# Window attention beside a gated feed-forward: the 8 KB transfer of the negated maxima is issued by GpSimd instead of SyncE

## The chip, the core and the metric

One core of one Trainium2 chip runs the whole program. The metric is the device time of one execution in microseconds; less is better. The time before is 872.02 us, the median of three runs (869.25 to 873.17).

## What is computed

The input x has 2048 tokens of 512 values. It is normed over each token, and two branches read the normed tokens:

```python
def _A_ref(x, wqkv, wo):            # 32 heads of 16, window of 256 tokens
    q, k, v = ...                   # x @ wqkv, split by head
    scores = jnp.einsum("bhqd,bhkd->bhqk", q, k) * (Dh ** -0.5)
    mask = (idx[:, None] - idx[None, :] >= 0) & (idx[:, None] - idx[None, :] < W)
    p = _softmax(jnp.where(mask[None, None], scores, -1e9), axis=-1)
    return (p @ v) @ wo
def _B_ref(x, w_gate, w_up, w_down):
    return (_silu(x @ w_gate) * (x @ w_up)) @ w_down
s = _A_ref(xn, A_wqkv, A_wo)
g = _silu(_B_ref(xn, B_w_gate, B_w_up, B_w_down))
return x + s * g
```

All data is float32.

## The kernel before

The tokens are cut into 4 chunks of 512. For each chunk the dense work on TensorE is: projections of queries and keys (tiles `a`), values (`vp`), gate and up (`g`, `u`), down (`d`) and the output projection (`s`). All of it goes through `next_mm`, and its matmuls stand on line 470. Each product is made of three, since every operand is split into a rounded part and a rest (`xh` and `xl`, `wh` and `wl`, `hh`). The rest of the weights, `wl`, is a GpSimd subtraction on line 434 that follows ScalarE's rounding on line 429. The rest of the hidden values, `hh`, is one on line 628.

Attention is made in 32 units u, 8 groups of 4 heads in each chunk. One unit goes through these steps:

1. `load_qk` brings its queries and keys from DRAM into the tiles `q` and `k` (SyncE's queue, tiles used in rotation by three).
2. `max_pair`: 16 score matmuls `b` (line 970), and for each a masked row maximum on VectorE (line 978) into one column of the tile `m`.
3. `max_turn`: two small transposes `mt` on TensorE (line 1004, first one half of the rows, then the other) turn the columns of maxima into rows.
4. `neg` (line 1019, ScalarE): the maxima, negated, go to the 16 x 128 tile `ms`. `put` then copies `ms` with one 8 KB DMA into row 48 and row 112 of the unit's `q` tile. Row 48 of the `k` tile holds ones, so that a product over 49 rows is score minus maximum.
5. `prob_pair`: matmuls `c` over 49 rows (line 1121), the exponential on ScalarE (`p`, line 1082), and the masks on the tile `p` by GpSimd (lines 1095 and 1099), one instruction for each masked block: 12 a unit in the first chunk, 16 in the others. The last two masks of a unit belong to its last pair of heads.
6. `pv_visit`: all products of `p` and `v` in one go (line 1158), which needs every mask of the unit.
7. The result goes to DRAM (`od`), is divided by the sums (`den`, `rd`) and comes back as the tile that `Wo` reads (`o`, lines 893 and 906).

The order of instructions on each engine is not written by hand. The program holds a planner, which runs while the kernel is built: it keeps a virtual clock, one queue of ready work for each of VectorE, ScalarE, GpSimd and DMA, and a cost for each piece. `do(engine, ready, cost, ...)` puts a piece in a queue and reports its end to a callback. `dma(...)` does the same for the queue of SyncE, with at most 8 transfers under way, a rate by size and 3.5 us (`LAND`) to landing. At each step the planner gives TensorE the dense matmul that is next, or an attention step whose inputs are ready by the virtual clock and whose due time has come. So a cost that is changed at one place changes the order of TensorE, ScalarE, VectorE, GpSimd and SyncE from there on. Each engine then runs its list in order on the chip, and waits on semaphores.

For the step at hand: `after_neg` is called when `neg` is done by the virtual clock. It queues `put`, and `ms_at[u]` is when the planner takes the maxima as landed. `prob_ready` asks for `ms_at[u]`, so it decides when the first `c` of the unit may be placed. The due times of `max_turn` and of the first `prob_pair` of a unit are 0.27 of a unit apart. The second transpose `mt` of unit u+1 (due at u + 1.8) stands close to `pv_visit` of unit u (due at u + 1.89).

Of the kernel before, what the change touches and what calls it, by code (L numbers as in the profile page):

```python
# [55 lines left out]
def tile_window_attention_swiglu_gate(  # L56
# [10 lines left out]
    nc = tc.nc  # L67
# [16 lines left out]
    def sb(name, shape, dtype, kind, n):  # L84
        return pers.tile(shape, dtype, name=name, tag=ring(kind, n), bufs=1)

    def f32(ap):
        return ap.bitcast(F32)

    def move(dst, src, eng=nc.sync):  # L90
        if dst.dtype == F32R:
            dst = f32(dst)
        if src.dtype == F32R:
            src = f32(src)
        eng.dma_start(dst, src)  # L95
# [11 lines left out]
    def do(e, ready, cost, fn, then=None, slack=0.5, can=None, lat=None):  # L107
        seq[0] += 1
        queue[e].append((ready + slack, seq[0], ready, cost, fn, then, can, LAT.get(e, 0.0) if lat is None else lat))
# [5 lines left out]
    def dma(ready, fn, then=None, slack=0.5, kb=256, can=None, e="D"):  # L115
        def begun_at(t):
            stream_at[0] = max(stream_at[0], t) + kb / 230.0
            done = stream_at[0] + LAND
            lanes.append(done)
            lanes.pop(0)  # L120
            if then:
                then(done)

        do(e, ready, 0.5, fn, begun_at, slack, lambda: lanes[0] <= now[0] and (can is None or can()), 0.0)
# [52 lines left out]
    def bank(pool, name):  # L177
        tag = min((v, k) for k, v in pool.items() if v is not None)[1]
        pool[tag] = None
        return ps.tile([P, 512], F32, name=name, tag=tag, bufs=1), tag  # L180
# [5 lines left out]
    qs = [pers.tile([P, 2, TC], F32R, name=f"q{i}") for i in range(3)]  # L186
# [168 lines left out]
    def half(r):  # L355
        return slice(R * r, R * r + R)
# [109 lines left out]
    def handover(pb):  # L466
        nc.vector.tensor_copy(pers.tile([MW, 1], F32, name="ho", tag=ring("ho", 2), bufs=1), pb[:MW, 0:1])
# [457 lines left out]
    ms_at = {}  # L925
# [72 lines left out]
    def max_turn(u, r):  # L998
        if r == 0:
            mtp[u] = [*bank(rb_free, f"mt{u}"), None]  # L1000
        pb, tag, _ = mtp[u]

        def go():
            nc.tensor.matmul(
                pb[:MW, R * r : R * r + R], mts[u % 2][half(r), :], ident[half(r), half(r)],
                is_transpose=True, start=True, stop=True,
            )

        if r == 0:
            def after(t):  # L1010
                mtp[u][2] = t

            extra[0].append((128, go, lambda t: do("V", t, 0.09, lambda: handover(pb), after, -1.0)))
            return
        box = []

        def neg():
            box.append(sb(f"ms{u}", [16, P], F32R, "ms", 2))
            nc.scalar.activation(box[0], pb[:16, :P], AF.Copy, scale=-1.0)

        def after_neg(t):
            rb_free[tag] = t
            dma(t, put, lambda t: ms_at.__setitem__(u, t + 1.0), -3.0, 8)

        def put():
            move(qs[u % 3][48 : 113 : 64], box[0])

        extra[1].append((128, go, lambda t: do("S", t, 0.25, neg, after_neg, -1.0)))

# [372 lines left out]
    while True:  # L1403
# [15 lines left out]
        if not any(extra):  # L1419
            s = work[0] / PACE - LEAD  # L1420
            for st in sorted(streams, key=lambda st: st[-1][0] if st else 1e9):
# [7 lines left out]
                t = need(*a)  # L1429
# [20 lines left out]
        if os.environ.get("VIRT"):  # L1450
            u, i = stream[min(pos[0], len(stream) - 1)]
# [40 lines left out]
```

## Time and profile before

| | us |
|---|---|
| median of three runs | 872.02 |
| the profiled execution, its time | 870.93 |
| its span on the core | 869.2 |
| TensorE matmul busy (PE) | 858.0 |
| GpSimd busy (POOL) | 638.1 |
| ScalarE busy (ACT) | 506.2 |
| VectorE busy (DVE) | 486.0 |

In the rows of the profile PE is TensorE's matmul, PEld its weight load, DVE VectorE, ACT ScalarE, POOL GpSimd, and SPq the queue of SyncE, which issues the DMAs. A row of the timeline has the start, the duration, the engine, the line, the operation, the tiles (out<-in, numbers left out), the shapes and a count; in brackets is the idle time of the engine before it, and what ended that. A row of the waits has the waiting instruction, what ended the wait, the sum in us, how often, and the longest. TensorE's clock was granted in full (0.999).

### The profile page before, as it was taken

What the parts mean: (1) busy time and instruction counts of PE and PEld (TensorE: products, weight loads), DVE (VectorE), ACT (ScalarE), POOL (GpSimd) and SP (SyncE); (2) the same over time, 40 slices, a digit from 0 to 9 for tenths busy, and PEclk for the clock granted to TensorE, in tenths of its full rate; (3) what the DMA queues carried; (4) which work ended last, traced back from release to release, by engine and by line L of the source; (5) the groups of instructions that cost most, each with busy time, mean ns of one, the idle gap of its engine ahead of it and who ended that gap; (6) DMA issues with size and microseconds to landing.
All of it is one profiled execution on the core that took longest, in us unless ns stands there. A gap on an engine that the chain in (4) does not pass through costs nothing.

```text
span 869.2 us, 30153 instructions
## 1 busy us (share of the span) xinstructions
PE 858.0 (99%) x11960; PEld 789.8 (91%) x11960; DVE 486.0 (56%) x1627; ACT 506.2 (58%) x1074; POOL 638.1 (73%) x888
## 2 busy tenths in 40 slices
PE   9999999999999999999999999999999999999997
PEld 8799999898889899989999989898999989999897
DVE  4364466655646655666555765565655566554233
ACT  4355565555665567565576666665656765566532
POOL 6576575668796776767799695676758997769774
PEclk9999999999999999999999999999999999999999
DMA  5785855466877985664767897556657779744342
GB/s 141 192 197 124 222 117 162 116 173 167 198 160 187 253 182 115 141 158 109 202 140 194 219 229 171 124 149 143 174 129 185 154 171 217 167 124 112 108 123 78
DMA packets 69489, 139.63 MB, mean 161 GB/s; under 512 B 14546, under 2 KB 23250, under 8 KB 69348
## 3 DMA queue, kind: packets, MB, share of 16 engines
q1 hardware_dynamic: 69060, 137.18, 63.9%
q8 instruction: 94, 1.54, 0.8%
q10 hardware_dynamic: 288, 0.52, 0.2%
q14 instruction: 47, 0.39, 0.2%
HBM read 107.74 MB, written 29.62 MB: 158 GB/s over the span
## 4 chain that ended last, share of the span: by engine, by line
PE 87%; DMA 8%; POOL 2%; SPq 1%; DVE 1%; issue 1%; ACT 1%; DVEq 0%; ACTq 0%; POOLq 0%
PE d L470 17%; PE u L470 15%; PE g L470 15%; PE a L470 11%; PE pv L1158 8%; PE s L470 5%; PE c L1121 5%; PE vp L470 4%; PE b L970 4%; DMA wr<-wo 2%; DMA k<-qkd 1%; POOL wl L434 1%; DMA den<-od 1%; DMA qkd<-qkl 1%; SPq L95 1%; DMA wr<-wqk 1%
## 5 line engine op out<-in xcount | busy, mean ns | idle before, releaser
L434 POOL TENSOR_TENSOR wl<-wr,wh 128x512 fp32r<-128x512 f32 (+2 forms) x258 | 306.8, 1207 | 101.1 <-ACT wh L429 91.9
L978 DVE CUSTOM_DVE_ANT_0 jk<-b,maskb 128x384 bf16<-128x384 f32 (+2 forms) x512 | 271.8, 531 | 132.5 <-PE b L970 71.5
L1082 ACT ACTIVATE p<-c 128x384 f32<-128x384 f32 (+1 forms) x480 | 208.2, 490 | 105.1 <-PE c L1121 89.0
L470 PE MATMUL d<-wh,hh 64*128 64x256 f32 x1792 | 259.3, 278 | 0.0
L470 PEld LDWEIGHTS d<-wh,hh 64*128 64x128 f32 x1792 | 227.1, 185 | 0.9 <-issue 0.6
L470 PE MATMUL d<-wl,hh 64*128 64x256 f32 x896 | 207.8, 279 | 0.0
L429 ACT ACTIVATE wh<-wr 128x512 fp32r<-128x512 f32 (+2 forms) x258 | 142.0, 594 | 65.5 <-PE d L470 16.0
L470 PE MATMUL u<-xh,wh 64*128 64x512 f32 x448 | 170.0, 396 | 0.0
L470 PE MATMUL g<-xh,wh 64*128 64x512 f32 x448 | 169.7, 395 | 0.0
L470 PE MATMUL u<-xl,wh 64*128 64x512 f32 x448 | 169.6, 396 | 0.0
L470 PE MATMUL g<-xl,wh 64*128 64x512 f32 x448 | 169.1, 395 | 0.0
L470 PE MATMUL u<-xh,wl 64*128 64x512 f32 x448 | 168.9, 395 | 0.0
L470 PE MATMUL g<-xh,wl 64*128 64x512 f32 x448 | 168.9, 395 | 0.0
L470 PEld LDWEIGHTS d<-wl,hh 64*128 64x128 f32 x896 | 154.9, 185 | 0.3
L1095 POOL TENSOR_SCALAR_AFFINE_SELECT p<-p 128x256 f32<-128x256 f32 x256 | 103.4, 408 | 57.1 <-ACT p L1082 54.0
L970 PE MATMUL b<-k,q 48*128 48x384 f32 (+1 forms) x512 | 116.6, 334 | 2.7 <-DMA k<-qkd 1.4
L1121 PE MATMUL c<-q,k 49*128 49x384 f32 (+1 forms) x704 | 111.7, 306 | 2.0 <-ACT p L1082 1.0
L1099 POOL TENSOR_SCALAR_AFFINE_SELECT p<-p 128x256 f32<-128x256 f32 x224 | 91.2, 409 | 11.4 <-ACT p L1082 9.6
L628 POOL TENSOR_TENSOR hh<-h,hh 128x512 fp32r<-128x512 f32 x56 | 72.5, 1295 | 36.4 <-ACT hh L624 30.1
L470 PE MATMUL a<-xh,wl 64*128 64x512 f32 (+1 forms) x264 | 97.0, 385 | 0.0
L470 PE MATMUL a<-xh,wh 64*128 64x512 f32 (+1 forms) x264 | 96.8, 390 | 0.0
L470 PE MATMUL a<-xl,wh 64*128 64x512 f32 (+1 forms) x264 | 96.1, 385 | 0.0
(102 smaller groups left out, 2109.6 us busy)
## 6 DMA issues: line engine op xcount, KB each, us to landing
wr<-wgu SPq DMA_DIRECT2D x112, 256.0 KB
k<-qkd SPq DMA_DIRECT2D x48, 192.0 KB
wr<-wqk SPq DMA_DIRECT2D x32, 256.0 KB
qkd<-qkh SPq DMA_DIRECT2D x32, 256.0 KB
qkd<-qkl SPq DMA_DIRECT2D x32, 256.0 KB
q<-qkd SPq DMA_DIRECT2D x64, 128.0 KB
wr<-wdn SPq DMA_DIRECT2D x32, 256.0 KB
od<-ev SPq DMA_DIRECT2D x32, 256.0 KB
```

Source lines behind the costliest of these rows:

```text
L95: eng.dma_start(dst, src)
L429: nc.scalar.activation(hi[0][pr, a:b], raw[pr, a:b], AF.Copy)
L434: nc.gpsimd.tensor_tensor(lo[0][pr, a:b], raw[pr, a:b], f32(hi[0][pr, a:b]), op=ALU.subtract)
L470: return nc.tensor.matmul(pb, a, b, start=first, stop=last, skip_group_check=True)
L628: nc.gpsimd.tensor_tensor(hl[:, 1, :], self.h, f32(hl[:, 0, :]), op=ALU.subtract)
L970: nc.tensor.matmul(pb[:, :w], qs[u % 3][r : r + 48, p, qb * P : (qb + 1) * P], ks[u % 3][r : r + 48, p, lo : lo + w], start=True, stop=True,)
L978: nc.vector.tensor_tensor_reduce(junk[:, :n], pb[:, :n], maskb[:, 3 * P - n :], 1.0, -3.0e38, ALU.add, ALU.max, m[:, col : col + 1],)
L1082: nc.scalar.activation(t[:, h, :], pc[:, a:b], AF.Exp, scale=DH ** -0.5)
L1095: nc.gpsimd.affine_select(s, s, [[0, 2], [1, P]], ALU.is_ge, 0.0, base=0, channel_multiplier=-1)
L1099: nc.gpsimd.affine_select(s, s, [[0, 2], [-1, P]], ALU.is_gt, 0.0, base=0, channel_multiplier=1)
L1121: nc.tensor.matmul(pc[:, at0 : at0 + w], ks[u % 3][r : r + 49, p, k0 : k0 + P], qs[u % 3][r : r + 49, p, qb * P : qb * P + w], start=(i == ...
L1158: nc.tensor.matmul(pbs[r][0][32 * j : 32 * j + 32, q0:q1], vt[half(r), (4 * c + kb) % VT, VW * (4 * g + j) : VW * (4 * g + j) + 32], t[hal ...
```

## The change

```diff
         def after_neg(t):
             rb_free[tag] = t
-            dma(t, put, lambda t: ms_at.__setitem__(u, t + 1.0), -3.0, 8)
+            do("G", t, 1.0, put, lambda t: ms_at.__setitem__(u, t + 2.0), -3.0)

         def put():
-            move(qs[u % 3][48 : 113 : 64], box[0])
+            move(qs[u % 3][48 : 113 : 64], box[0], nc.gpsimd)
```

`put` is now issued on GpSimd's own queue, between GpSimd's other instructions and in their order, with a wait for `neg`. The planner books 1.0 us of GpSimd for it and takes the maxima as landed 2.0 us after that (and the 0.12 us that it adds to each piece of GpSimd), where it had a turn in SyncE's queue, one of 8 places, 3.5 us and 1.0 us. The 32 instructions leave SyncE's list. No other instruction is added or removed; TensorE has the same 10,528 matmuls of 3,574,784 columns in all. Their order differs from unit 0 on.

Three places of the new order. The first is TensorE's list behind the second transpose of unit 0; `c_0_0` and `c_0_1` are the first products over 49 rows of unit 0, `g_4` and `vp_0_0` dense tiles. Rows with + are new at this place.

```order
 L470 MATMUL g_4_751<-xh_79,wh_646 128x512
 L470 MATMUL vp_0_0_839<-wh_646,xl_80 128x256
+L1121 MATMUL c_0_0_852<-q_72,k_75 128x256
+L1121 MATMUL c_0_1_853<-q_72,k_75 128x256
+L1121 MATMUL c_0_0_852<-q_72,k_75 128x256
+L1121 MATMUL c_0_1_853<-q_72,k_75 128x256
 L470 MATMUL vp_0_0_839<-wh_646,xh_79 128x256
 L470 MATMUL g_4_751<-xl_80,wh_646 128x512
```

From the second transpose of unit 0 to its first `c` stood 76 matmuls of 31,488 columns; now 43 of 20,224. In 26 of the 32 units the first `c` has moved closer to the transpose, in 3 it stands where it was (units 12, 23 and 25), in 3 it is further (17, 28 and 31).

The second place is GpSimd's list around the last masks of unit 8, the first unit of the second chunk. In the order before, four masks of unit 8 stand in a row:

```order
L434 TENSOR_TENSOR wl_4842<-wr_4601,wh_4841 128x512 x2
L1095 AFFINE_SELECT p<-p 128x2x128
L1099 AFFINE_SELECT p<-p 128x2x128
L1095 AFFINE_SELECT p<-p 128x2x128
L1099 AFFINE_SELECT p<-p 128x2x128
L434 TENSOR_TENSOR wl_4962<-wr_4768,wh_4961 128x512 x2
```

In the order of the change the transfer of unit 9 stands between them:

```order
L434 TENSOR_TENSOR wl_4841<-wr_4658,wh_4840 128x512 x2
L1095 AFFINE_SELECT p<-p 128x2x128
L1099 AFFINE_SELECT p<-p 128x2x128
L95 DMA q_72<-ms_4931 2x8x128
L1095 AFFINE_SELECT p<-p 128x2x128
L1099 AFFINE_SELECT p<-p 128x2x128
L434 TENSOR_TENSOR wl_4964<-wr_4837,wh_4963 128x512 x2
```

The last two masks of unit 8 now come behind a DMA that waits for `neg` of unit 9. TensorE's list has moved with it: from the second transpose of unit 9 to `pv` of unit 8 stood 9,472 columns, now 12,544. In 12 units (8, 9, 15 to 18, 20, 25 to 28 and 30) the DMA of the next unit stands ahead of the last masks of the unit in this way.

The third place is the same engine at unit 9. In the order before, the last two masks follow a sum for the output of the first chunk (`y`, line 829):

```order
L434 TENSOR_TENSOR wl_5319<-wr_5050,wh_5318 128x512 x2
L1095 AFFINE_SELECT p<-p 128x2x128
L1099 AFFINE_SELECT p<-p 128x2x128
L829 TENSOR_TENSOR y_0_0_5358<-y_0_0_5358,xr_0_0_5141 128x512
L1095 AFFINE_SELECT p<-p 128x2x128
L1099 AFFINE_SELECT p<-p 128x2x128
```

In the order of the change the transfer of unit 10 comes ahead of them:

```order
L1099 AFFINE_SELECT p<-p 128x2x128
L829 TENSOR_TENSOR y_0_0_5359<-y_0_0_5359,xr_0_0_5140 128x512
L95 DMA q_73<-ms_5446 2x8x128
L1095 AFFINE_SELECT p<-p 128x2x128
L1099 AFFINE_SELECT p<-p 128x2x128
```

From the second transpose of unit 10 to `pv` of unit 9 stood 6,656 columns, now 11,264. In the other ten of the 12 units, other work has changed places on GpSimd too.

## The prediction

> **What bounds the kernel now.** The page comes first, for the share of each engine and for where GpSimd is full.
>
> ```profile
> span 869.2 us, 30153 instructions
> PE 858.0 (99%) x11960; PEld 789.8 (91%) x11960; DVE 486.0 (56%) x1627; ACT 506.2 (58%) x1074; POOL 638.1 (73%) x888
> POOL 6576575668796776767799695676758997769774
> ```
>
> TensorE is busy for 858.0 of 869.2 us, all along. GpSimd is next with 73%, and its slices 20, 21, 23, 31 and 36 are at nine tenths, so there it has little room. TensorE does the same 3,574,784 columns after the change, so what can change is the 11.2 us in which it is idle. The waits of TensorE say what those are:
>
> ```profile
> PE b L970 <- DMA k<-qkd: 1.4, 1, 1.4
> PE warm L236 <- DVE warm L231: 1.1, 1, 1.1
> PE c L1121 <- ACT p L1082: 1.0, 1, 1.0
> PE b L970 <- ACT p L1082: 1.0, 2, 0.5
> PE c L1121 <- DMA q<-ms: 0.8, 1, 0.8
> PE s L470 <- issue: 0.5, 1, 0.5
> PE b L970 <- DVE m L978: 0.3, 1, 0.3
> ```
>
> One of them is the transfer in question: 0.8 us, once in 32 units. The timeline at that place (unit 8), TensorE's rows and the issue in SyncE's queue:
>
> ```profile
> 231.90 0.60 SPq L95 DMA_DIRECT2D q<-ms  x1
> ...
> 239.84 0.74 PE L1121 MATMUL c<-q,k 49*128 49x256 f32 x8 [0.76 <-DMA q<-ms]
> ```
>
> So there the 8 KB took 7.9 us from issue to landing. In the other 31 units TensorE doesn't wait for it: it has other work between the transpose and the first `c`.
>
> The second tie is not in that list, because it shows at the weight loads of `pv`:
>
> ```profile
> PEld pv L1158 <- issue: 4.2, 14, 0.4
> PEld pv L1158 <- POOL p L1099: 2.0, 6, 0.4
> PEld pv L1158 <- POOL hh L628: 0.7, 2, 0.4
> ```
>
> Of the 32 visits 22 waited, never over 0.4 us: `pv` starts as soon as the last mask is made. From the second chunk on there is no margin between GpSimd's masks and TensorE. Unit 8 row by row, with the transpose and the negation of unit 9 ahead:
>
> ```profile
> 255.19 0.22 PE L1004 MATMUL mt<-ident,m 64*80 64x64 f32 x1
> ...
> 255.49 0.27 ACT L1019 ACTIVATE ms<-mt 16x128 fp32r<-16x128 f32 x1 [0.42 <-PE a L470]
> ...
> 256.15 0.42 POOL L1099 TENSOR_SCALAR_AFFINE_SELECT p<-p 128x256 f32<-128x256 f32 x1
> 256.51 0.42 POOL L1095 TENSOR_SCALAR_AFFINE_SELECT p<-p 128x256 f32<-128x256 f32 x1
> 256.87 0.42 POOL L1099 TENSOR_SCALAR_AFFINE_SELECT p<-p 128x256 f32<-128x256 f32 x1
> ...
> 257.61 0.50 PE L1158 MATMUL pv<-p,v 64*32 64x320 f32 x8
> ```
>
> The last mask ends at 257.29 and `pv` starts at 257.61. A microsecond of GpSimd placed ahead of these masks would be a microsecond of TensorE if TensorE's list had not moved too.
>
> **The change, part by part.** The scale between list and time is 858.0 us for 3,574,784 columns, 0.240 ns a column.
>
> *Removed from SyncE's list.* 32 issues, and waits for `neg` that held up what stood behind them; ahead of their rows is the one wait of TensorE for a large transfer:
>
> ```profile
> 38.24 0.39 PE L970 MATMUL b<-k,q 48*128 48x256 f32 x2 [1.37 <-DMA k<-qkd]
> ...
> SPq L95 <- ACT ms L1019: 18.6, 10, 3.9
> ...
> L95 SPq DMA_DIRECT2D q<-ms x32: 553/600/1432, 52.1 to 787.7; - x32
> ```
>
> That is 32 x 0.60 = 19 us of issue and 18.6 us of waiting on a queue for whose large transfers TensorE waits once, at 38.24, at the first `b` of unit 0 and ahead of the change. I count the relief of the queue at nothing. The wait of unit 8 goes, if the transfer no longer stands behind the large ones of SyncE: -0.8 us.
>
> The rule against that is the Trainium skill's, DMA: Bandwidth & Descriptors, section "Issuing engines are not separate DMA queues": transfers of all issuers run on the same 16 DMA engines and interleave, and another issuer saves only the time of the issue. By it the 0.8 us would stay; no row here has a second issuer beside a full queue, so the trace can't decide.
>
> *TensorE's list: `c` is asked for sooner.* In 26 units the first `c` has moved towards the transpose. The shortest distances are unit 0 with 20,224 columns (4.85 us) and unit 3 with 19,968 (4.79 us). What has to fit in is GpSimd's work ahead of the DMA, the DMA's time on GpSimd, and its landing. No row has a transfer issued by GpSimd. The nearest is a small transfer of SyncE, 16 KB, which was issued and already used 3.30 us later; the bounds are an issue alone (0.55, the shortest above) and unit 8's 7.9.
>
> ```profile
> 444.44 0.65 SPq L95 DMA_DIRECT2D den<-od  x1
> ...
> 447.74 0.35 DVE L866 RECIPROCAL den<-den 128x32 f32<-128x32 f32 x1
> ```
>
> I take 3.3 us from issue to landing. Unit 0:
>
> ```profile
> 50.49 0.21 PE L1004 MATMUL mt<-ident,m 64*80 64x64 f32 x1
> ...
> 51.45 2.54 POOL L434 TENSOR_TENSOR wl<-wr,wh 128x512 fp32r<-128x512 f32 x2 [3.77 <-ACT wh L429]
> ...
> 51.80 0.25 ACT L1019 ACTIVATE ms<-mt 16x128 fp32r<-16x128 f32 x1
> ```
>
> The DMA stands behind the first of the two `wl`, so it can start at 51.45 + 1.27 = 52.72 (the negation is done at 52.05) and land at 56.02. TensorE comes to `c` at 50.49 + 4.85 = 55.34. That is a wait of 0.7 us. Unit 3:
>
> ```profile
> 118.36 0.21 PE L1004 MATMUL mt<-ident,m 64*80 64x64 f32 x1
> ...
> 118.88 0.25 ACT L1019 ACTIVATE ms<-mt 16x128 fp32r<-16x128 f32 x1
> ...
> 120.21 1.30 POOL L434 TENSOR_TENSOR wl<-wr,wh 128x512 fp32r<-128x512 f32 x1 [2.09 <-ACT wh L429]
> ```
>
> There the negation was done at 119.13 and GpSimd was idle, so: 119.13 + 3.3 = 122.43, and TensorE comes at 118.36 + 4.79 = 123.15, with 0.7 us to spare. The next shortest are unit 5 with 23,552 columns, 5.65 us, and unit 6 with 24,064; with a start between 0.8 us (unit 3) and 2.2 us (unit 0) behind the transpose they have room for 3.3 us. New waits at `c`: +0.7 us.
>
> *GpSimd's list: 32 transfers more.* In 20 units the DMA stands behind the masks of the unit before, and what it delays is `wl` or `hh`, which TensorE never waits for in the list above; I count these at nothing. In the other 12 it stands ahead of the last masks, and the planner has moved `pv` back for it, by 3,072 columns in unit 8 (0.74 us) and 4,608 in unit 9 (1.11 us). Whether that is enough depends on the time X for which the transfer holds GpSimd. Unit 8: the negation is done at 255.76, GpSimd can turn to the DMA at 256.51, the masks end at 257.29 + X; `pv` comes at 255.19 + 12,544 columns (3.01) = 258.20. So X up to 0.9 us costs nothing. Unit 9:
>
> ```profile
> 278.44 1.29 POOL L829 TENSOR_TENSOR y<-y,xr 128x512 f32<-128x512 f32 x1
> 279.69 0.40 POOL L1095 TENSOR_SCALAR_AFFINE_SELECT p<-p 128x256 f32<-128x256 f32 x1
> 280.05 0.40 POOL L1099 TENSOR_SCALAR_AFFINE_SELECT p<-p 128x256 f32<-128x256 f32 x1
> ...
> 279.04 0.21 PE L1004 MATMUL mt<-ident,m 64*80 64x64 f32 x1
> ```
>
> Masks end at 280.45 + X, `pv` comes at 279.04 + 11,264 columns (2.70) = 281.74: X up to 1.3 us is free. The mean of the two is 1.1, and I use it for all 12: the cost is 12 x (X - 1.1), if X is above that. The nearest rows for X are SyncE's issues of this very transfer, 0.55 to 1.43 us. I take the middle, 1.0, which is also what the planner books: +0.1 us (unit 8 alone). At 0.55 it is nothing, at 1.43 it is 12 x 0.33 = 4.0.
>
> The Trainium skill, same page, section "Specifications", has a first byte from GpSimd's path at about 1 us and from SyncE's at about 0.6 us, so it speaks against the move. An estimate from that page's fixed cost of about 2.0 us for a whole DMA (section "Anatomy of one DMA") would drop the wait of unit 0, and the sum below would be 0.7 us less.
>
> *Other waits.* The list has moved everywhere behind unit 0, so the 1.0 + 1.0 + 0.3 us for `p` and `m` will fall elsewhere; I count them the same. At the end TensorE has the same work:
>
> ```profile
> 852.74 11.76 PE s L470 x150
> ```
>
> That ends at 864.5, and 4.7 us of last sums and stores follow.
>
> **The sum.** 870.93 (the profiled execution; its span is 869.2) - 0.8 + 0.7 + 0.1 = 870.9. The median of the runs is 1.1 us above that execution, so the forecast for the median is 870.9 + 1.1 = 872.0: no change. A measurement of this kernel can tell about 0.5%, 4.4 us, so faster is below 867.7 and slower above 876.4.
>
> **The rivals.**
>
> *GpSimd becomes the bound at the masks (slower).* If X is longer than what `pv` was moved back, each of the 12 units passes the rest to TensorE, since 22 of 32 visits already wait for the masks. At X = 1.6 it is 12 x 0.5 = 6.0 us: 878.0. It decides the sign from X = 1.1 + 4.4/12 = 1.47 on. For: the zero margin at `pv`, and GpSimd's full slices. Against: the slowest of the 32 issues on SyncE took 1.43. Chance 0.25.
>
> *The landing is late (slower).* At 5.0 us from issue to landing unit 0 waits 52.72 + 5.0 - 55.34 = 2.4 and unit 3 119.13 + 5.0 - 123.15 = 1.0 us. With a start 1.3 us behind the transpose, units 5, 6, 8, 1, 7, 13 and 2, with 5.65, 5.78, 5.84, 6.02, 6.02, 6.08 and 6.21 us by their columns, wait 2.5 in all. That is 5.9 instead of 0.7: 877.2. For: unit 8's 7.9 us. Against: that one stood behind large transfers in one queue. Chance 0.10.
>
> *The new list loses its waits (faster).* Of 11.2 us of idle time 1.1 and 1.4 lie ahead of the change and 4.7 behind the last matmul, which leaves 4.0: 868.0 if all went. For more than 0.5% TensorE's own rows would have to shrink; their ends are modelled, so it can't be excluded. Chance 0.12.
>
> *The transfer is moved and lands no sooner.* The move then does not do what it says, unit 8's wait of 0.8 us stays, and the time is 872.8. Chance 0.08. The rule on issuing engines named above is of this kind.
>
> The forecast keeps 0.45. Low is 867.5, just below the rival that loses all waits; high is 881.0, which takes in X up to 1.85 and the late landing. Faster gets 0.1 (most of the third rival, as its 868.0 is next to the line), slower 0.3 (nearly all of the first and most of the second), same 0.6.
>
> **What would show it.** The row of `q<-ms` on GpSimd gives X: near 1.0 by the forecast, 1.5 or more by the first rival. The loads of `pv` should wait no more than the 6.9 us of now, and with the first rival by some 0.5 us in each of the 12 units. TensorE's `c` should wait for `q<-ms` once, in unit 0, and not in unit 8. I am wrong if the idle time of TensorE leaves 11 us by more than 4, or if TensorE's busy time itself moves.

## The result, and the profile after

The changed kernel takes 880.25 us in the median of six runs, the kernel before 870.27 us in six runs on the same chip: 1.0116 of before, with a 95% interval of 1.009 to 1.0142. It is slower. The forecast was 872.0 us, no change; its range (867.5 to 881.0) just holds the result. Further down, one execution each of `land4` (1493.6 us), `r_both` (883.5 us) and the kernel before (1683.3 us) was in a slower state and stands in no ratio. The profiled execution took 879.3 us, with a span of 877.6 us, next to 870.93 and 869.2 before.

The page of the changed kernel, as it was shown of before:

```profile
span 877.6 us, 30131 instructions
PE 858.5 (98%) x11960; PEld 797.7 (91%) x11960; DVE 484.8 (55%) x1627; ACT 505.8 (58%) x1074; POOL 657.3 (75%) x920
```

TensorE's busy time is 858.5 us and was 858.0. So of the 8.4 us by which the span grew, 7.9 are idle time of TensorE: 877.6 - 858.5 = 19.1 us, and 11.2 before. GpSimd is busy for 19.2 us more in 32 more instructions. What TensorE waits for:

```profile
PE c L1121 <- DMA q<-ms: 7.4, 5, 2.6
PE b L970 <- DMA k<-qkd: 1.5, 2, 1.3
PE c L1121 <- ACT p L1082: 1.5, 2, 1.3
...
```

The first row was 0.8 us, once. It is 7.4 us in five units now, which is 6.6 of the 7.9 us of added idle time. By the timeline the five are units 0, 8, 14, 19 and 26 (unit 8's row comes below):

```profile
59.23 0.50 PE L1121 MATMUL c<-q,k 49*128 49x256 f32 x4 [1.85 <-DMA q<-ms]
...
390.88 0.51 PE L1121 MATMUL c<-q,k 49*128 49x256 f32 x4 [1.29 <-DMA q<-ms]
...
514.49 0.56 PE L1121 MATMUL c<-q,k 49*128 49x256 f32 x4 [0.99 <-DMA q<-ms]
...
682.77 0.50 PE L1121 MATMUL c<-q,k 49*128 49x256 f32 x4 [0.68 <-DMA q<-ms]
```

The answer on the tile `ms` (the first row has the shortest, middle and longest time of the issue on GpSimd, in ns; the last has the time from issue to landing):

```profile
L95 POOL DMA_DIRECT2D q<-ms x32: 575/575/787, 54.7 to 795.9; - x32
...
DMA to landing us min/median/max: 1.7/4.1/7.9
```

So the transfer holds GpSimd for 0.575 us and lands 4.1 us after its start in the middle case, up to 7.9. The weight loads of `pv`, which would have shown GpSimd as the bound, wait about as long as before (7.1 us in all next to 6.9, 0.4 us at most); the two largest rows are:

```profile
PEld pv L1158 <- issue: 3.9, 12, 0.4
...
PEld pv L1158 <- POOL p L1099: 1.8, 5, 0.4
```

The costliest place is unit 8 again. Its transpose, its issue and its first products in the timeline, with the transfer of `r` (the reciprocals of the softmax sums), GpSimd's product `o` that waits for it, and ScalarE's `oh` that waits for the product, in the same microseconds:

```profile
233.48 0.62 SPq L95 DMA_DIRECT2D r<-rd  x1
...
234.89 0.25 PE L1004 MATMUL mt<-ident,m 64*80 64x64 f32 x1 [0.86 <-DVE ho L467]
...
235.74 0.60 POOL L95 DMA_DIRECT2D q<-ms  x1
...
241.97 1.26 POOL L893 TENSOR_TENSOR o<-o,r 128x512 f32<-128x512 f32 x1 [4.31 <-DMA r<-rd]
243.26 0.63 ACT L903 ACTIVATE oh<-o 128x512 fp32r<-128x512 f32 x1 [3.44 <-POOL o L893]
...
243.74 0.80 PE L1121 MATMUL c<-q,k 49*128 49x256 f32 x4 [2.56 <-DMA q<-ms]
```

The transfer was issued 0.85 us after the transpose began, but landed 7.9 us later, as in SyncE's queue before. The list asks for `c` 24,320 columns (5.84 us) behind the transpose. After the wait, TensorE does not come back at full speed. In the table by windows, each row has the window, its length, the busy time of PE, PEld, DVE, ACT and POOL with their counts, and then the granted clock of TensorE:

```profile
241.00:243.50 2.50, 0.17 (x1) 0.00 (x0) 0.41 (x2) 0.24 (x1) 1.53 (x2) 0.99 0.80 212
243.50:246.90 3.40, 3.17 (x18) 2.90 (x20) 0.62 (x3) 2.60 (x6) 3.40 (x3) 0.50 0.23 77
246.90:250.00 3.10, 3.10 (x34) 2.74 (x32) 2.20 (x7) 0.66 (x2) 2.75 (x6) 1.00 0.00 0
```

For 3.4 us the clock is 0.50, and 18 matmuls are done where the next 3.1 us hold 34. These 1.7 us show as busy time, not as a wait. (Over the whole span the busy time grew by only 0.5 us, so other places gave some of it back.)

### The profile page after: what moved, and what is told of

Same layout as the page of the kernel before. It is cut to its first block, busy times and chain, and to the rows that moved or that the text cites. A ratio compares the mean times of both kernels' runs of the same rounds, so it can differ in the third digit from the quotient of the medians.

```text
span 877.6 us, 30131 instructions
## 1 busy us (share of the span) xinstructions
PE 858.5 (98%) x11960; PEld 797.7 (91%) x11960; DVE 484.8 (55%) x1627; ACT 505.8 (58%) x1074; POOL 657.3 (75%) x920
## 4 chain that ended last, share of the span: by engine, by line
PE 84%; DMA 9%; POOL 3%; issue 1%; ACT 1%; DVE 1%; SPq 0%; ACTq 0%; POOLq 0%; DVEq 0%
PE d L470 17%; PE u L470 16%; PE g L470 15%; PE a L470 10%; PE pv L1158 7%; PE c L1121 5%; PE s L470 5%; PE vp L470 4%; PE b L970 4%; DMA q<-ms 4%; POOL wl L434 2%; DMA xt<-x 1%; DMA r<-rd 1%; DMA wr<-wo 1%; DMA wr<-wqk 1%
## 5 line engine op out<-in xcount | busy, mean ns | idle before, releaser
L470 PE MATMUL d<-wh,hh 64*128 64x256 f32 x1792 | 263.6, 278 | 0.0
L470 PE MATMUL g<-xl,wh 64*128 64x512 f32 x448 | 166.6, 395 | 0.0
L470 PE MATMUL u<-xl,wh 64*128 64x512 f32 x448 | 166.5, 396 | 0.0
L470 PE MATMUL g<-xh,wh 64*128 64x512 f32 x448 | 166.2, 396 | 0.0
L470 PE MATMUL u<-xh,wh 64*128 64x512 f32 x448 | 166.1, 397 | 0.0
L470 PE MATMUL g<-xh,wl 64*128 64x512 f32 x448 | 165.3, 395 | 0.0
L470 PEld LDWEIGHTS d<-wl,hh 64*128 64x128 f32 x896 | 152.3, 185 | 0.2
L1121 PE MATMUL c<-q,k 49*128 49x384 f32 (+1 forms) x704 | 117.0, 306 | 8.8 <-DMA q<-ms 7.4
L1121 PEld LDWEIGHTS c<-q,k 49*128 49x128 f32 x704 | 87.1, 186 | 14.5 <-issue 5.6
L470 PE MATMUL a<-xh,wh 64*128 64x512 f32 (+1 forms) x264 | 99.5, 397 | 0.0
```

The source lines that it names most:

```text
L470: return nc.tensor.matmul(pb, a, b, start=first, stop=last, skip_group_check=True)
L1121: nc.tensor.matmul(pc[:, at0 : at0 + w], ks[u % 3][r : r + 49, p, k0 : k0 + P], qs[u % 3][r : r + 49, p, qb * P : qb * P + w], start=(i == ...
```

## The experiments

The theories at the start: **booking** (the planner now believes in a landing 3.1 us behind the transfer's turn, where it was 4.5, places the first `c` closer, and the chip's landing is later) against **issuer** (GpSimd's queue, its time and its path cost it). The edits were 16 small variants; each ratio below is to the kernel before, run on the same chip, with its 95% interval.

### The issuer alone, and the booking alone

The list of before, with the transfer issued by GpSimd (`e1_issuer`):

```diff
-            move(qs[u % 3][48 : 113 : 64], box[0])
+            move(qs[u % 3][48 : 113 : 64], box[0], nc.gpsimd)
```

> The kernel before with one thing changed: the 8 KB transfer is issued in GpSimd's queue, and the planner books it as it did before (a turn in SyncE's virtual queue, 3.5 us to landing and 1.0 more). TensorE's list is the one of before, matmul for matmul; only the issuer differs. Theory A (the booking: the first c is placed for a landing 2.0 us after the issue, and the landing takes 1.7 to 7.9 us): the distances from the transpose to the first c are those of before, 6.2 us or more, so c waits for q<-ms once or twice, at most 3 us, and the time is that of before within 0.5%: 868 to 874. Theory B (the issuer: GpSimd's queue lands later than SyncE's and holds GpSimd ahead of masks that pv waits for): slower by most of the measured 1.2%, 876 to 882, with waits of c for q<-ms as in the changed kernel (7.4 us), or of pv for the masks over 0.4 us.

And the list of the change, with the transfer issued by SyncE (`e2_booking`, the other half of the diff):

> The changed kernel with one thing undone: the transfer is issued in SyncE's queue again, and the planner books it as in the change. TensorE's list is the one of the change, matmul for matmul, with the first c 4.8 us behind the transpose at the shortest and 6.8 in the middle. Theory A (the booking): as slow as the change or slower, 878 to 890, since SyncE's queue has its own backlog; c waits for q<-ms in five units or more, 7 us or more in all. Theory B (the issuer): the time of before within 0.5%, 868 to 874, and few waits at c.

Measured: the issuer alone 1.0037 [1.0018, 1.0057], the booking alone 1.0164 [1.0144, 1.0184]. TensorE's waits at `c`, first with the issuer alone, then with the booking alone:

```profile
PE c L1121 <- DMA q<-ms: 0.9, 1, 0.9
```

```profile
PE c L1121 <- DMA q<-ms: 12.1, 5, 4.0
```

The wait comes with the list, whichever engine issues. The 0.9 us of the first run are unit 8, as before: a queue of its own did not make that landing sooner. GpSimd issued the transfer 2.29 us behind the transpose, SyncE had done so after 0.92 us, and the first `c` could start 8.95 us behind the transpose, next to 8.86 before.

Which units wait does depend on the issuer: 0, 8, 14, 19 and 26 in the changed kernel, 0, 8, 10, 16 and 26 with the same list and SyncE. At units 10 and 16 other transfers stood ahead in SyncE's list, so it issued this one 4.3 and 4.9 us behind the transpose, where GpSimd did so after 1.0 and 1.4 us. Unit 16 with SyncE, where the list asks for `c` 7.2 us behind the transpose:

```profile
433.40 0.21 PE L1004 MATMUL mt<-ident,m 64*80 64x64 f32 x1
...
438.27 0.55 SPq L95 DMA_DIRECT2D q<-ms  x1
...
444.85 0.80 PE L1121 MATMUL c<-q,k 49*128 49x256 f32 x4 [4.00 <-DMA q<-ms]
```

In the run with SyncE, TensorE's stops were long enough for two stretches of half clock in a row (granted clock behind the five counts):

```profile
440.50:443.00 2.50, 0.35 (x5) 0.14 (x2) 0.69 (x1) 0.84 (x2) 1.98 (x2) 0.98 0.79 263
443.00:446.40 3.40, 1.55 (x12) 1.58 (x14) 0.00 (x0) 0.69 (x3) 2.97 (x3) 0.50 0.99 289
446.40:449.80 3.40, 3.40 (x29) 3.40 (x28) 1.73 (x5) 2.05 (x5) 2.83 (x5) 0.51 0.71 143
```

### More distance, with GpSimd as issuer

The changed kernel with a later landing in the planner's books, first 5.0 us, then 8.0, 4.0 and 6.0 (`land5`, `land8`, `land4`, `land6`):

```diff
-            do("G", t, 1.0, put, lambda t: ms_at.__setitem__(u, t + 2.0), -3.0)
+            do("G", t, 1.0, put, lambda t: ms_at.__setitem__(u, t + 5.0), -3.0)
```

> The change with one number raised: the planner takes the maxima as landed 5.0 us after GpSimd's 1.0 us for the transfer, not 2.0. The first c stands 6.6 us behind the transpose at the shortest, 8.2 in the middle. With the landing times of the changed kernel, unit by unit, c would wait 0.1 us in all. Theory A (the booking): the loss goes, 866 to 874. Theory B (the issuer): the GpSimd queue still costs, 876 or more.

> The same with 8.0 us: the first c stands 9.6 us behind the transpose at the shortest, 11.2 in the middle, over every landing seen (7.9 us at most). Theory A (the booking): no wait of c for q<-ms at all; what is left is the luck of a new list, 865 to 876, and a second effect may show, that the later softmax of a unit comes into conflict with its due times. Theory B: 876 or more.

> The change with the landing booked at 4.0 us after GpSimd's 1.0, between the 2.0 of the change and the 5.0 that took the loss away. The first c stands 6.1 us behind the transpose at the shortest, 7.6 in the middle; with the landing times of the changed kernel c would wait 1.8 us in three units (10, 19, 26). Theory A: 868 to 873, c waits for q<-ms 1 to 3 us. Theory B (issuer or luck of the list): anything between 870 and 882, without relation to the waits at c.

> The same with 6.0 us: 7.8 us at the shortest, 9.0 in the middle; no wait of c for q<-ms. Theory A with a far side (a booking far over the landing pushes the softmax of a unit into its neighbours, as at 8.0 us, where products b and c stood alone on TensorE at 271 to 274 us and 10.2 us at half clock followed): 868 to 874, if that far side begins between 6 and 8. If it is a matter of luck at one place, it may be anywhere from 866 to 880.

Measured: 1.0044 [1.0015, 1.0073] at 4.0, 1.0021 [1.0003, 1.0038] at 5.0, 1.0038 [1.0014, 1.0062] at 6.0 and 1.0122 [1.0105, 1.0138] at 8.0. The wait for the landing falls to 1.0 us or less at 4.0 and 5.0 and is gone from 6.0 on (the profiled execution at 4.0, 866.9 us, was the fastest of its run, so the others may have waited more); other waits come in its place. At 6.0 the largest is that of `c` for `p`, 4.2 us in two pieces. At 8.0, slower than the 865 to 876 us that the booking theory expected, the loss is mainly at one place: between 264 and 275 us TensorE is given only 66 matmuls in 11 us, where the 9 us ahead held 158, and then the clock is half for 10 us:

```profile
255.00:264.00 9.00, 9.00 (x158) 7.43 (x156) 3.94 (x15) 3.81 (x8) 5.98 (x9) 1.00 0.42 116
264.00:270.00 6.00, 6.00 (x43) 5.14 (x40) 3.05 (x9) 3.45 (x8) 3.67 (x5) 1.00 0.72 213
270.00:275.00 5.00, 3.92 (x23) 2.66 (x22) 3.38 (x11) 3.94 (x8) 4.21 (x8) 0.96 0.63 209
275.00:280.00 5.00, 5.00 (x26) 5.00 (x25) 0.72 (x3) 0.00 (x0) 0.81 (x3) 0.50 0.81 245
280.00:285.00 5.00, 5.00 (x41) 5.00 (x42) 0.15 (x1) 0.75 (x2) 0.00 (x0) 0.51 0.86 211
```

### The landing without a reader

In the list of the change, the transfer goes to a spare tile from unit 3 on, so that no product waits for it (`no_reader`):

```diff
-            move(qs[u % 3][48 : 113 : 64], box[0], nc.gpsimd)
+            move(qs[u % 3][48 : 113 : 64] if u < 3 else warm[:16], box[0], nc.gpsimd)
```

> The changed kernel, with every list as it is, but from unit 3 on the transfer goes to a tile that is done with (16 x 128 of the warm-up tile), so that no product waits for its landing; the rows that the products read keep the maxima of units 0 to 2. GpSimd issues it at the same place and waits for the negation as before. Theory A (waits of c for a landing that was booked too short): the waits of units 8, 14, 19 and 26 go, 5.3 of the 7.4 us, and with them the 3.4 us stretch of half clock behind unit 8's (1.7 us); unit 0's stays; 870 to 875 against 880 for the change. Theory B (GpSimd held up, or the luck of a list with c and pv in other places): no gain, 878 to 882.

Measured: 1.0099 [1.0066, 1.0133], a miss for the booking theory as it stood. The wait for the landing went (1.3 us are left, in unit 0), and the time stayed. TensorE's idle time fell by only 2.2 us, to 16.9, and its busy time rose by 2.1, to 860.6: between 30 and 870 us it has four stretches at half clock (from 40, 245, 296 and 443 us on), and the changed kernel has one. TensorE's waits:

```profile
PE s L470 <- issue: 3.5, 2, 1.9
PE c L1121 <- ACT p L1082: 3.5, 2, 2.0
...
PE c L1121 <- DMA q<-ms: 1.3, 1, 1.3
```

The stops at 391 and 683 us are gone. At 244 us TensorE stops again, now 2.0 us for ScalarE's `p`, at 442 us for `p` as in the changed kernel, and at 295 and 516 us for something that the profile does not name. At unit 8 the timeline of this run says why. The first `c` comes at 239.56, and the first `p` that reads one comes 4 us later:

```profile
239.56 0.28 PE L1121 MATMUL c<-q,k 49*128 49x256 f32 x1
...
240.86 1.28 POOL L893 TENSOR_TENSOR o<-o,r 128x512 f32<-128x512 f32 x1 [4.48 <-DMA r<-rd]
...
242.18 0.63 ACT L903 ACTIVATE oh<-o 128x512 fp32r<-128x512 f32 x1 [3.57 <-POOL o L893]
243.10 0.63 ACT L429 ACTIVATE wh<-wr 128x512 fp32r<-128x512 f32 x1 [0.29 <-DMA wr<-wv]
...
243.63 0.37 ACT L1082 ACTIVATE p<-c 128x256 f32<-128x256 f32 x1
```

The list has `oh` ahead of `p`, `oh` waits for GpSimd's product, and that product waits for the landing of `r`. In the list of before the four `p` stand ahead of this `oh`:

```profile
240.35 1.21 ACT L1082 ACTIVATE p<-c 128x256 f32<-128x256 f32 x4 [0.48 <-PE c L1121]
242.75 0.63 ACT L903 ACTIVATE oh<-o 128x512 fp32r<-128x512 f32 x1 [1.19 <-POOL o L893]
```

So the new list meets two late landings in the same microseconds. Whether the second keeps the loss was the next question. GpSimd multiplies `o` by itself, so that nothing waits for `r`; in the list of the change, in that of `no_reader`, and in the list of before as the base (`r_after`, `r_both`, `r_before`):

```diff
-            nc.gpsimd.tensor_tensor(box[0], box[0], box[1], op=ALU.mult)
+            nc.gpsimd.tensor_tensor(box[0], box[0], box[0], op=ALU.mult)
```

> The list of the change with two landings unread: from unit 3 on the maxima go to a spare tile, and POOL multiplies o by itself instead of by the reciprocal sums r, so that it does not wait for the landing of r (the output is not the reference's). The transfers and every engine's order stay. Theory T, two landings late at the same places: TensorE's stops near 244 and 442 us go, the loss falls from 1.0 per cent to 0 to 0.6. Theory U, a third input (weights, banks) is as late: 0.8 to 1.1 per cent stay.

> The changed kernel with the maxima read as they are, but POOL multiplying o by itself, so that r's landing is not waited for (the output is not the reference's). Theory T: little changes while the maxima's landing stands there, 0.7 to 1.2 per cent over the kernel before, with 5 us or more of waits for it at c. If the reciprocal sums were the whole of it: 0 to 0.4 per cent.

> The kernel before with POOL multiplying o by itself, so that nothing waits for r's landing (the output is not the reference's): the base for the two others. In the profile of before ACT's oh waits 8.7 us for POOL but TensorE waits for none of it: 0.997 to 1.001. If it falls to 0.995 or less, the gain of r_both is no sign of the change's list.

Measured: without either landing 1.0051 [1.0028, 1.0075], without `r`'s alone 1.0111 [1.0084, 1.0138], the base 0.998 [0.9962, 0.9998]. With only one of the two landings taken away, the other holds the time (in `r_after` the wait for the maxima is 7.9 us in five units). Against its own base without `r`, the list of the change is 1.0131, and 1.0071 without both: with `r` out of the way, taking the maxima's landing away as well saves about half of the loss, where it saved only 0.2% with `r` in place (1.0116 to 1.0099). That is between the two theories: the intervals of `r_both` and `no_reader` overlap a little, TensorE's stop at unit 8 is 1.9 us from the start of one matmul to the start of the next, where it was 2.4, and the one near 445 us is no shorter (2.1 us, 1.8 in `no_reader`). ScalarE at unit 8, in the run without either landing:

```profile
241.48 0.63 ACT L903 ACTIVATE oh<-o 128x512 fp32r<-128x512 f32 x1 [1.48 <-POOL o L893]
243.97 0.63 ACT L429 ACTIVATE wh<-wr 128x512 fp32r<-128x512 f32 x1 [1.85 <-DMA wr<-wv]
244.51 0.36 ACT L1082 ACTIVATE p<-c 128x256 f32<-128x256 f32 x1
```

A third landing, that of a weight, stands behind the two. Taking that one away was not tried. The base `r_before` has such stops too: in its profiled execution `c` waits 3.0 us for the maxima of unit 10, which SyncE's queue issued 5.2 us behind the transpose.

### Distance on SyncE's queue

If it is the distance, SyncE's queue must show it too. The kernel before with other bookings (`sp_0`, `sp_2`, `sp_23`, `sp_3` have 0.0, 2.0, 2.3 and 3.0):

```diff
-            dma(t, put, lambda t: ms_at.__setitem__(u, t + 1.0), -3.0, 8)
+            dma(t, put, lambda t: ms_at.__setitem__(u, t + 2.0), -3.0, 8)
```

> The kernel before, its transfer in SyncE's queue, with one number raised: the maxima are taken as landed 2.0 us after the booked landing, not 1.0. The first c stands 6.8 us behind the transpose at the shortest, 8.8 in the middle (6.2 and 8.0 before). Theory A: unit 8's wait of 0.8 us goes and nothing else changes on purpose: 866 to 870, the only candidate here to beat the kernel before. Theory B has no say: the issuer is that of before.

> The kernel before with the transfer still asked for by SyncE, booked to land 1.0 us earlier than before (t + 0.0 in place of t + 1.0). Its first product of a unit stands 7.0 us of dense columns behind the transposed maxima in the middle case and 5.0 in the shortest, next to 6.8 and 4.8 in the changed kernel and 8.0 and 6.2 before, and it is a list of its own. Theory A, the distance decides: the first product waits for its landing at several units, 3 to 8 us of waits, and the time is 0.5 to 1.2 per cent above the kernel before. Theory L, it is the one list of the changed kernel that happens to run badly at a few places, and the distance is only one of many inputs: no relation to the distance, within 0.4 per cent of the kernel before.

> The run with SyncE and the landing booked 1.0 us later than before, with 0.3 us more (t + 2.3): distance 9.2 us in the middle and 7.1 in the shortest case, and a third of TensorE's rows in another place. Theory A, every landing is covered and the rest is as good: 0.995 to 0.998 of the kernel before. Theory L, the 0.9961 was a lucky list: 0.999 to 1.005.

> SyncE's queue and a landing booked 2.0 us later than before (t + 3.0): distance 9.9 us in the middle and 7.9 in the shortest case. Theory A, past the longest landing more distance brings nothing: 0.996 to 0.999. If the dense work that has to stand ahead runs short as with the landing booked at 8.0 us on GpSimd (11.2 and 9.6): 1.000 to 1.006.

Two controls went with them. `hold06` books GpSimd at 0.6 us and the landing at 2.4 us: the landing is believed at the same time as in the change, in another list.

> The changed kernel with GpSimd booked for 0.6 us instead of 1.0 and the landing for 2.4 us instead of 2.0, so that the landing is expected at the same time while POOL's price is nearer to the measured 0.575 us: another list at the same distance (6.7 us middle, 4.8 shortest). Theory A: the loss stays, 0.8 to 1.4 per cent above the kernel before, with 5 to 12 us of waits for the landing at c. Theory L: the loss belongs to the one list, so 0 to 0.6 per cent.

`sp2_gp` is the list of `sp_2` issued by GpSimd.

> The list of the run in which SyncE issues the transfer and it is booked 1.0 us later than before (0.9961 of the kernel before), the transfer now issued by GpSimd; the order of every engine but SP and POOL stays. Theory B, the issuer costs something by itself, as the list of before with GpSimd showed (1.0037): 0.4 per cent above the run with SyncE, so 1.000 of the kernel before. Theory A, the issuer costs nothing and that 1.0037 was the wait of unit 8 and scatter: 0.996 to 0.998, with no wait for the landing.

All the lists, by the distance from the second transpose to the first `c` (their columns at 0.240 ns):

| run | issuer | booked | distance, middle / shortest, us | ratio to before |
|---|---|---|---|---|
| `hold06` | GpSimd | 0.6 + 2.4 | 6.7 / 4.8 | 1.0282 [1.0241, 1.0323] |
| the change | GpSimd | 1.0 + 2.0 | 6.8 / 4.8 | 1.0116 [1.009, 1.0142] |
| `e2_booking` | SyncE | as the change | 6.8 / 4.8 | 1.0164 [1.0144, 1.0184] |
| `sp_0` | SyncE | t + 0.0 | 7.0 / 5.0 | 1.0087 [1.0054, 1.0121] |
| `land4` | GpSimd | 1.0 + 4.0 | 7.6 / 6.1 | 1.0044 [1.0015, 1.0073] |
| before | SyncE | t + 1.0 | 8.0 / 6.2 | 1 |
| `e1_issuer` | GpSimd | as before | 8.0 / 6.2 | 1.0037 [1.0018, 1.0057] |
| `land5` | GpSimd | 1.0 + 5.0 | 8.2 / 6.6 | 1.0021 [1.0003, 1.0038] |
| `sp_2` | SyncE | t + 2.0 | 8.8 / 6.8 | 0.9961 [0.9938, 0.9984] |
| `sp2_gp` | GpSimd | as `sp_2` | 8.8 / 6.8 | 0.9991 [0.9972, 1.001] |
| `land6` | GpSimd | 1.0 + 6.0 | 9.0 / 7.8 | 1.0038 [1.0014, 1.0062] |
| `sp_23` | SyncE | t + 2.3 | 9.2 / 7.1 | 0.9962 [0.9943, 0.9981] |
| `sp_3` | SyncE | t + 3.0 | 9.9 / 7.9 | 0.9991 [0.9972, 1.0011] |
| `land8` | GpSimd | 1.0 + 8.0 | 11.2 / 9.6 | 1.0122 [1.0105, 1.0138] |

All four kernels (three lists) with a shortest distance of 5.0 us or less lose 0.9 to 2.8%, with either issuer; from 6.1 to 7.9 us of shortest distance all stay within 0.5% of before; 9.6 us is too much. The best are `sp_2` and `sp_23`, 865.64 and 866.38 us, two lists with SyncE that both beat the kernel before and the changed one. The page and the waits of `sp_2`:

```profile
span 863.0 us, 30158 instructions
PE 854.4 (99%) x11960; PEld 790.5 (92%) x11960; DVE 483.8 (56%) x1627; ACT 505.2 (59%) x1074; POOL 637.8 (74%) x888
```

```profile
PE warm L236 <- DVE warm L231: 1.1, 1, 1.1
PE mt L1004 <- DVE ho L467: 0.8, 1, 0.8
PE b L970 <- DMA k<-qkd: 0.7, 1, 0.7
PE c L1121 <- ACT p L1082: 0.5, 1, 0.5
...
```

No `c` waits for the transfer. TensorE is idle for 8.6 us instead of 11.2 and busy for 3.6 us less in the same columns.

`sp_0` lost as expected, but by other waits than expected:

```profile
PE c L1121 <- ACT oh L903: 3.2, 1, 3.2
PE c L1121 <- ACT p L1082: 1.8, 1, 1.8
...
PE c L1121 <- DMA q<-ms: 0.7, 2, 0.5
```

The largest is at unit 8 and has `oh` in it, the second late input of above. `hold06` lost more than either theory had said: 11.7 us of waits for the landing at six `c`, and a clock below full at four places. How much a short distance costs hangs on the list; all four kernels that have one lose. That they lose by waiting for the maxima shows in the rows of the change, `e2_booking` and `hold06`; in `sp_0` only 0.7 us are such waits, and the short distance brought other late inputs out.

GpSimd as issuer costs 0.4% in the list of before (1.0037, at least 0.2% by its interval), some 3 us. The pair `sp2_gp` and `sp_2` agrees with that, 0.9991 to 0.9961, which is 1.0030, but the two were run on different chips and their intervals overlap, so it does not show it by itself. In the profiles of `sp_2` and `sp2_gp` these microseconds lie at many places, and no stop of TensorE is above 1.3 us in either; what carries them is not settled. With the change's own list the order of the two is the other way (1.0116 and 1.0164), in separate sets of runs. There SyncE's late issues at units 10 and 16 stand against GpSimd's cost: 12.1 us of waits at `c` next to 7.4.

## Why the prediction failed, step by step

*What bounds the kernel* held: TensorE is busy for the same time, and the loss is idle time and clock.

*The step that failed is "new waits at `c`: +0.7 us"*, a wait of 0.7 us in unit 0 alone. It measured 7.4 us in five units. The mechanism, a first `c` that comes ahead of its landing, was right for the waits, and their size was not; the time hangs on more than this one landing (`no_reader` below).

- Unit 0's own term was mis-sized only by the landing. Taken were a start 2.23 us behind the transpose and 3.3 us; measured, the transfer is issued 2.28 us behind it (54.72 against 52.44) and lands 4.38 us later. With 4.38 for 3.3 the sum gives 0.7 + 1.08 = 1.8 us; the wait is 1.85.
- Unit 3 had 0.7 us to spare by the prediction, and just made it: landed at 126.98, first `c` at 127.12.
- Units 8, 14, 19 and 26 took 7.86, 6.24, 6.38 and 6.50 us to land. Their distances are 5.8, 6.9, 7.1 and 7.7 us; the last three stood in no sum, not even in that of the rival with a late landing. One landing time was used for 32 units. The profile of before had a second figure, unit 8's 7.9 us, and it was put down to SyncE's queue. The changed kernel's 7.9 us, and the wait of 0.9 us that stays in `e1_issuer`, speak against that. A spread from 3.3 to 7.9, laid over all 32 distances, would have reached these units; it would not have told them from the many others that are as close and did not wait.

*Unit 8's wait goes, -0.8 us* failed: the landing took 7.9 us again, and the wait rose to 2.6 us. The rule of the Trainium skill that spoke against this term (DMA: Bandwidth & Descriptors, "Issuing engines are not separate DMA queues") agrees with the trace here: with one list, unit 8's `c` waits 0.9 us when GpSimd issues and 0.8 when SyncE does.

*The relief of SyncE's queue at nothing* held with the old list: `e1_issuer` has the relief, and no gain. With the new list it had a worth: in `e2_booking`, without it, units 10 and 16 wait 6.7 us for the maxima, and in the changed kernel they don't.

*The masks, X = 1.0 us, +0.1 us*: X is 0.575 us, the price was nothing, and the loads of `pv` wait 7.1 us, next to 6.9 before. The rival with the largest chance (0.25, GpSimd as the bound) is refuted at this place. But the 0.4% of a GpSimd issuer were in no term. (The slices of GpSimd at nine tenths are seven, 11, 20, 21, 23, 31, 32 and 36 when counted from 0, and not five; no term rests on that.)

*The other waits stay the same* failed by some 1.3 us in the sum (7.9 - 6.6), and in kind: `no_reader` and `r_both` show that `p` and `oh` are late at unit 8 too and only hidden behind the landing. The prediction counted each wait as if its removal freed TensorE.

*No term for the clock.* A stop of TensorE of 2 us or more can bring 3.4 us of half clock, another 1.7 us, which the waits do not show; in the changed kernel unit 8 paid it.

*The rivals.* The late landing (chance 0.10, 877.2 us) was the right one for the waits, with 5.9 us at `c` against 7.4, in partly other units; that `no_reader` keeps the time without them was in no rival. The list that loses its waits (faster) did not come with the change, but `sp_2` shows that such a list exists; its gain is in TensorE's own busy time too, as that rival had left open.

*The range* held 880.25 by luck: 881.0 was set for an X of up to 1.85 us, and X was 0.575. The prediction's own sign of being wrong did come, TensorE's idle time left 11 us by more than 4 (19.1).

## What to carry to other kernels

A transfer's price in a planner is its landing under the load of its place, and that is a spread (here 1.7 to 7.9 us for the same 8 KB in one execution, and 8.5 us once in `hold06`), not a number: lay the longest landing seen over every consumer before believing that a shorter booking is free, and try the booking by itself before the engine that issues. When one late input is taken away and the time stays, look for what else is late at that place; here a second landing stood behind the first, and a third, not tested, behind both. A stop of TensorE can be dearer than the row of the waits says, because the clock can fall behind it.

## What the hardware showed that was not expected

**Half clock after short stops.** TensorE's granted clock fell to 0.5 for 3.4 us, or twice that, after stops of 2.40, 2.92, 2.96, 3.34 and 4.28 us, each from the start of one matmul to the start of the next (`e2_booking` and the changed kernel), and in `no_reader` after one of 1.76 us, where 3.5 us hold 30 matmuls and the next 3.0 us hold 50:

```profile
442.50:446.00 3.50, 3.50 (x30) 3.50 (x28) 1.88 (x6) 1.39 (x5) 3.50 (x5) 0.52 0.84 212
446.00:449.00 3.00, 3.00 (x50) 3.00 (x49) 1.80 (x6) 2.39 (x5) 2.63 (x6) 0.99 0.48 131
```

Stops of 2.24 and 1.69 us in the changed kernel did not bring it, nor did one of 3.57 us in `hold06`; 11 us with few matmuls in `land8` did. The Trainium skill (TensorE: Matmul & The Clock Gate, section "HAM oscillation — how this bites in real kernels") gives the rule "no PE-idle gaps >~3.4µs". The length of 3.4 us agrees with its window, but shorter stops were enough here, so that the rule is no safe margin.

**GpSimd's issue is short, its landing not.** 0.575 us on the engine, near that on SyncE's queue (0.600 in the middle), and 1.7 to 7.9 us to landing from the same source tile to the same kind of tile. In the longest landing (unit 8) the 16 DMA engines were busy 0.87 of the time, in the shortest (unit 30) 0.03.

**The same booking, unequal times.** `hold06` and the change believe in the same landing and differ by 1.6%. A planner's list has a spread of its own, so the gain of 0.4% was believed here only when two lists (`sp_2` and `sp_23`) showed it.
